# Delta-rule attention with a gated convolution: T's natural layout by identity products on PE, the first group's 16-to-32 step as PE products, and a redrawn order

## The chip, the cores and the metric

The kernel runs on one core of one Trainium2 chip. The metric is device time in microseconds (us) of the whole launch. Shown beside it is the span of the profiled execution, from the first to the last instruction in its trace. PE is the matrix engine (TensorE), DVE the vector engine, ACT the scalar engine, POOL GpSimd, SP the engine that issues the transfers; PEld is PE's weight load.

## The reference

For each of 4 batches and 8 heads a state of 48 x 48 is carried over 768 positions. Each position reads the state with its query, and then corrects the state by a delta rule along its normalised key; the outputs of the heads are put side by side to rows of 384 and go through a gate of a causal convolution of 5 taps, a value product, and an output product.

```python
k_n = k / (norm(k, axis=-1) + 1e-6)
for t in range(S):                                    # S = 768
    y[t]  = q[t] @ state                              # 48 x 48 state per batch and head
    state = state + b[t] * outer(k_n[t], v[t] - k_n[t] @ state)
x = y, heads side by side                             # 4 x 768 x 384
gate = sigmoid(sum over k of conv_w[k] * x[t - 4 + k])
out  = (gate * (x @ w_val)) @ w_out
```

The three weight arrays of the second half arrive as 64-bit floats and are turned to 32 bits on the chip.

## The kernel before

The positions are cut into 12 chunks of 64, and two chunks make a group, so there are 6 groups, numbered 0 to 5. 32 pairs of batch and head are handled at once; in a group there are 32 columns `u`, 16 for each chunk `c` (0 and 1), and each column carries two pairs on the halves of the 128 partitions.

**Preparing a group (`prep`).** `gram` multiplies keys with keys and queries (tile KQ, loaded by SP) on PE, and ACT copies the result to GL. `diag` copies the diagonal 32 x 32 blocks to D1, and a DVE transpose turns them into TLP. `coef` works out the norms and, with the loaded beta (tile BE), the factors CT: its 18th step is the first that reads BE, and everything behind it needs CT. Inside one chunk of 64 the delta rule needs the inverse T of a unit triangular matrix. DVE builds it for blocks of 8 (`row`), merges them to 16 (`mergez8`, `merget8`), and then to 32 (`zmul`, `zred`, `tmul`, `tred`; POOL does a part of the products). All of this has the 128 matrices' entries along the free dimension. `trans_out(0)` then transposes to the layout TTR, and `trans_out(1)` a second time to TNA, the natural (not transposed) layout of T. Last, the step from 32 to 64 is done on PE: `lev1` multiplies GL and TTR into a bank `z`, ACT copies it to ZS (four copies of 32 partitions), `lev2` multiplies TNA and ZS into a bank `t`, and ACT copies it into BD beside two scaled copies of TTR (`bdcopy`).

**Following the state (`chain`).** For each chunk the products `e` (state with keys, KF), `u` (BD with the corrected values VT), `S` (update of the state, kept in the PSUM tiles SPS) and `y` (output) run on PE, with ACT and DVE copying between. `y` goes to XB, a part of it through YS and six small transfers.

**The second half (`moe`).** For each chunk and each of three blocks `m` of 128 features: `conv` does taps 0 and 1 on PE, DVE adds taps 2 to 4 (`tap`), ACT applies the sigmoid, `val` (three products) and `gate` follow, then `out` (two runs of three products), a copy to OS, and the store. POOL copies four positions from one chunk's X to the next (`halo`).

**What sets the order.** All operations are recorded by `plan.add` in a list. They are then issued in the sequence of a table of numbers, `ORDER`; an operation keeps to its place on its engine, since every engine works in order. So a load that stands late in the table stands late in SP's queue. -1 in the table is a `keep_warm`: one product of zeros with zeros into SPS0, which changes no result. The trace shows each 32-bit product as two records, and counts so: 147 keep-warm products are 294 records. The banks of the pool `w` (3 banks: gram, z, t, val, out) and of the pool `c` (3 banks: conv, e, u, y) go round.

The weights of the second half are loaded in seven pieces through two staging slots that lie in other tiles (AQ1, XB1, GTB0), and converted by two ACT, four DVE and two POOL operations each (lines 273 to 290).

## Time and profile before

| | |
|---|---|
| median of 3 runs | 338.1 us (337.85, 338.10, 345.43) |
| profiled execution, own time | 338.18 us |
| its span | 336.5 us |
| busy, share of the span | PE 308.9 us (92%), DVE 261.8 (78%), ACT 193.3 (57%), POOL 124.7 (37%) |
| instructions of the span | 13,878 |
| DMA | 39.47 MB, 117 GB/s in the mean |

The profiled execution's own time is 1.7 us above its span and 0.1 us above the median. A row of the timeline reads: start, duration, engine, line, operation, result <- operands, the shapes, and how many instructions were merged; in square brackets the idle time before it and what ended it. A row of the view by windows reads: the stretch, its length, then for PE, PEld, DVE, ACT and POOL the busy time and the instructions, then the granted PE clock as a share of full speed, the share of the DMA engines' time, and GB/s. A row of the view by groups reads: busy time, mean ns of one instruction, and the idle time before them.

### The profile page before, as it was taken

How to read it: one execution, taken by the hardware profiler on the slowest of the kernel's cores; microseconds unless marked ns; L12 is line 12 of the kernel's file. 1: busy time of each engine (PE TensorE's matmuls, PEld its weight loads, DVE VectorE, ACT ScalarE, POOL GpSimd, SP SyncE). 2: the span in 40 equal slices, each digit the busy share in tenths (PEclk: the TensorE clock that was granted, in tenths of full speed). 3: DMA queues.
4: the chain of work that ended last, by engine and by line, in shares of the span. 5: the costliest groups of instructions: out<-in, count | busy, mean ns of one | idle time of the engine just before them, and what ended most of it. 6: DMA issues, size and time to landing. Idle time of an engine off the chain costs nothing.

```text
span 336.5 us, 13878 instructions
## 1 busy us (share of the span) xinstructions
PE 308.9 (92%) x6050; PEld 251.0 (75%) x6050; DVE 261.8 (78%) x565; ACT 193.3 (57%) x428; POOL 124.7 (37%) x92
## 2 busy tenths in 40 slices
PE   8936999699779979999999999999999999999994
PEld 6835899589757868777787887868776787786872
DVE  5368999999698994999997899896998779511640
ACT  6742402987636865598455897534875633575221
POOL 5441355244980005960057620485200583300000
PEclk9987599755997998999999999999999999999999
DMA  7899805045440573625087664014341742301222
GB/s 213 265 205 262 191 0 158 3 113 170 128 123 1 137 185 113 179 59 159 15 222 209 186 131 150 8 57 131 107 115 37 204 109 79 96 4 27 47 47 47
DMA packets 20283, 39.47 MB, mean 117 GB/s; under 512 B 8112, under 2 KB 11312, under 8 KB 20224
## 3 DMA queue, kind: packets, MB, share of 16 engines
q1 hardware_dynamic: 20224, 38.60, 43.5%
q8 instruction: 47, 0.77, 1.0%
q14 instruction: 12, 0.10, 0.1%
HBM read 32.69 MB, written 4.72 MB: 111 GB/s over the span
## 4 chain that ended last, share of the span: by engine, by line
PE 60%; DVE 14%; ACT 8%; DMA 7%; POOL 4%; issue 3%; SPq 3%; POOLq 0%; ACTq 0%; DVEq 0%
PE out L726 14%; PE val L715 11%; PE conv L700 7%; PE gram L358 4%; PE e L581 4%; PE u L581 3%; PE SPS L769 3%; PE y L649 3%; SPq L221 3%; PE SPS L581 2%; PE y L651 2%; PE z L458 2%; DMA AQ<-in_w_val_dram 2%; PE t L478 2%; DMA X<-YS 2%
## 5 line engine op out<-in xcount | busy, mean ns | idle before, releaser
L705 DVE SCALAR_TENSOR_TENSOR conv<-X,CW,conv 128x256 f32<-128x256 f32 x108 | 49.9, 484 | 14.2 <-PE conv L700 12.1
L715 PE MATMUL val<-X,WV 128*128 128x256 f32 x216 | 52.5, 390 | 0.0
L726 PE MATMUL out<-WO,GT 128*128 128x384 f32 x144 | 50.9, 495 | 0.0
L421 POOL TENSOR_TENSOR PR<-TLP,TT__83 128x768 f32<-128x768 f32 x5 | 10.6, 2118 | 97.0 <-DVE TT__83 L416 97.0
L715 PEld LDWEIGHTS val<-X,WV 128*128 128x128 f32 x216 | 40.3, 192 | 6.9 <-ACT GL L216 0.3
L769 PE MATMUL SPS<-ZW 128*128 128x128 f32 x294 | 43.7, 302 | 0.4 <-ACT US L643 0.4
L769 PEld LDWEIGHTS SPS<-ZW 128*128 128x128 f32 x294 | 39.4, 210 | 5.1 <-issue 3.6
L358 PE MATMUL gram<-KQ 48*64 48x128 f32 x768 | 33.4, 311 | 10.2 <-DMA KQ<-in_kq_dram 8.5
L700 PE MATMUL conv<-X,DW 128*128 128x256 f32 x144 | 37.5, 396 | 2.7 <-POOL X L695 2.3
L726 PEld LDWEIGHTS out<-WO,GT 128*128 128x128 f32 x144 | 26.2, 189 | 15.0 <-DVE GT L719 0.2
L216 ACT ACTIVATE GL<-gram 128x512 f32<-128x512 f32 x48 | 27.1, 596 | 16.7 <-PE gram L358 16.2
L358 PEld LDWEIGHTS gram<-KQ 48*64 48x64 f32 x768 | 26.1, 156 | 13.6 <-issue 9.3
L649 PE MATMUL y<-AQ,US 112*64 112x64 f32 x384 | 31.0, 237 | 4.7 <-issue 4.0
L649 PEld LDWEIGHTS y<-AQ,US 112*64 112x64 f32 x384 | 26.8, 147 | 8.9 <-issue 7.7
L700 PEld LDWEIGHTS conv<-X,DW 128*128 128x128 f32 x144 | 26.5, 194 | 8.4 <-POOL X L695 2.7
L559 POOL TENSOR_SCALAR_AFFINE_SELECT AQ<-GL 64x1024 f32<-64x1024 f32 x24 | 29.2, 1216 | 7.2 <-PE y L649 3.5
L216 ACT ACTIVATE D<-GL 32x512 f32<-32x512 f32 (+1 forms) x36 | 22.6, 628 | 15.8 <-DVE TT__83 L441 15.1
L581 PE MATMUL u<-VT,BD 64*64 64x48 f32 x768 | 30.6, 233 | 0.7 <-DVE VT L633 0.6
L581 PEld LDWEIGHTS u<-VT,BD 64*64 64x64 f32 x768 | 27.7, 148 | 3.8 <-issue 1.1
L651 PE MATMUL y<-AQ,US 128*48 128x64 f32 x384 | 29.1, 233 | 0.0
L633 DVE TENSOR_TENSOR VT<-e,VT 128x384 f32<-128x384 f32 x22 | 12.3, 557 | 20.1 <-PE e L581 14.1
L637 ACT ACTIVATE US<-u 64x384 f32<-64x384 f32 x24 | 11.6, 483 | 27.9 <-PE u L581 27.8
(97 smaller groups left out, 609.7 us busy)
## 6 DMA issues: line engine op xcount, KB each, us to landing
KQ<-in_kq_dram SPq DMA_DIRECT2D x24, 448.0 KB, 5.6
KF<-in_kf_dram SPq DMA_DIRECT2D x11, 448.0 KB, 4.6
KT<-in_kt_dram SPq DMA_DIRECT2D x12, 384.0 KB, 4.2
AQ<-in_qf_dram SPq DMA_DIRECT2D x24, 192.0 KB, 4.5
VT<-in_vt_dram SPq DMA_DIRECT2D x12, 384.0 KB, 4.0
out_dram<-OS SPq DMA_DIRECT2D x48, 96.0 KB, 2.7
AQ<-in_w_val_dram SPq DMA_DIRECT2D x3, 384.0 KB, 6.0
AQ<-in_w_out_dram SPq DMA_DIRECT2D x3, 384.0 KB, 7.6
```

The lines of the kernel that those rows point to most:

```text
L216: A.activation(out=out, in_=in_, func=AF.Copy, **kw)
L358: PE.matmul(bank["g", g, c, 2 * h + s][64 * a:64 * a + 64, 128 * j:128 * (j + 1)], x[:, 0:C], x, start=True, stop=True)
L559: G.affine_select(out=AQ[c][r0:r0 + 64, j], in_=GL[r0:r0 + 64, c * NP:(c + 1) * NP, 64:128], pattern=[[0, NP], [1, C]], compare_op=ALU.is_ ...
L581: return lambda: PE.matmul(*a, stop=True, **k)
L633: V.tensor_tensor(out=v, in0=bank["e", ch, h][:, 0:HB * D].rearrange("p (u x) -> p u x", x=D), in1=v, op=ALU.add)
L649: PE.matmul(p[0:64, C * j:C * j + C], US[ch % 3][0:112, 0, h, D * j:D * j + 64], AQ[c][0:112, 0, pp, :], start=True, stop=True)
L651: PE.matmul(p[64:112, C * j:C * j + C], us[:, 1, h, j, :], AQ[c][:, 1, pp, :], start=True, stop=True)
L700: PE.matmul(p[:, 0:B * C].rearrange("p (b t) -> p b t", t=C), DW[:, m, i, :], x[:, m, :, k:k + C], start=(i == 0), stop=(i == len(PTAPS) - 1))
L705: V.scalar_tensor_tensor(out=p, in0=x[:, m, :, k:k + C], scalar=CW[:, m, k:k + 1], in1=p, op0=ALU.mult, op1=ALU.add)
L715: PE.matmul(p[:, 0:B * C].rearrange("p (b t) -> p b t", t=C), WV[:, k, 128 * m:128 * m + 128], xs[:, k], start=(k == 0), stop=(k == NKT - 1))
L726: PE.matmul(bank["o", ch, i][:, 0:DM], GT[k][:, 2 * i:2 * i + 2, :].rearrange("p b t -> p (b t)"), WO[:, k, :], start=(k == 0), stop=(k == ...
L769: PE.matmul(SPS[0][:, 384:512], ZW, ZW, start=False, stop=True, skip_group_check=True)
```

## The change

T's natural layout is no longer made by DVE's second transpose in groups 1 to 5. PE multiplies blocks of TTR with 32 x 32 pieces of the identity (`lev0`, bank `n`), and ACT copies the bank to TN; there is such a run for each chunk of each group, group 0 too. TN and ZS now hold two halves of 64 partitions, so that one ACT copy of 128 x 256 fills ZS where four of 32 x 256 did, and `lev2` reads and writes on the diagonal places of the array.

In group 0 (`MERGE = (0,)`) DVE stops at blocks of 16. The half-merged T is transposed to TTR and to TNA (so here the second transpose stays), PE multiplies GL with the second half of TTR (`mergew`, 128 products, bank `mw`), DVE turns the bank into WI by a mask and an identity (`mergew_evac`), PE multiplies TNA with WI (`mergeq`, 128 products, bank `mq`), and ACT copies the result into the second half of TTR. The 16-to-32 products of POOL and DVE are gone from this group. POOL builds the two small constants IDH and ML at the start. The other five groups keep DVE's and POOL's 16-to-32 step as it was.

The table `ORDER` is written anew. It holds 86 keep-warm products (147 before). PTAPS stays (0, 1), so that the new branches for no taps on PE are not taken.

```diff
+MERGE = (0,)
 ORDER = [
-    -1, 8, 16, 65, 160, 9, 70, -1, 3, 1, 2, 7, 75, -1, 10, 11, 12, -1, 13, -2, 14, 17, 0, 4, 6, -1, 15, 24, 64, 18,
...
+    -1, 66, 17, 9, 299, 71, 76, 107, 67, 68, 151, 18, 10, 19, 11, 12, 13, 20, 14, 15, 69, 70, 6, 2, 16, 5, 21, 22,
...
+        def mergew(c):
+            if c == 0:
+                bank["mw", g] = wps("mw")
+            for u in range(c * NP, (c + 1) * NP):
+                for r in range(0, 128, 32):
+                    PE.matmul(bank["mw", g][r:r + 32, 16 * u:16 * u + 16], GL[r:r + 32, u, r % 64:r % 64 + 32],
+                              TTR[r:r + 32, u, 16:32], start=True, stop=True, tile_position=(r, r))
+
+        def mergew_evac():
+            V.scalar_tensor_tensor(
+                out=WI, in0=bank["mw", g].rearrange("p (u x) -> p u x", x=16), scalar=ML[:, 0:1],
+                in1=IDH.unsqueeze(1).to_broadcast([128, NU, 16]), op0=ALU.mult, op1=ALU.add)
+
+        def mergeq(c):
+            if c == 0:
+                bank["mq", g] = wps("mq")
+            for u in range(c * NP, (c + 1) * NP):
+                for r in range(0, 128, 32):
+                    PE.matmul(bank["mq", g][r:r + 32, 16 * u:16 * u + 16], TNA[r:r + 32, u, :], WI[r:r + 32, u, :],
+                              start=True, stop=True, tile_position=(r, r))
+
+        def mergeq_evac():
+            copy(A, TTR[:, :, 16:32], bank["mq", g].rearrange("p (u x) -> p u x", x=16))
+
+        def lev0(c):
+            p = bank["n", g, c] = wps("n")
+            for pp in range(NP):
                 u, x = c * NP + pp, 32 * (pp // 2)
                 for r in (0, 64):
-                    to = r + 32 * (pp % 2)
+                    to = 64 * (pp % 2) + r // 2
+                    PE.matmul(p[to:to + 32, x:x + 32], TTR[r:r + 32, u, :], EYE[r:r + 32, r:r + 32],
+                              start=True, stop=True, tile_position=(r, to))
+
+        def nevac(c):
+            copy(A, TN, bank["n", g, c][:, 0:256].rearrange("p (u x) -> p u x", x=32))
...
         def zevac(c):
-            for r in (0, 64):
-                for b in range(2):
-                    copy(A, ZS[r:r + 32, b:NP:2], bank["z", g, c][r + 32 * b:r + 32 * b + 32, 0:256].rearrange("p (u x) -> p u x", x=32))
+            copy(A, ZS, bank["z", g, c][:, 0:256].rearrange("p (u x) -> p u x", x=32))
...
-        def lev2(c, h):
...
+        def lev2(c):
...
                 for r in (0, 64):
-                    to = r + 32 * (pp % 2)
-                    PE.matmul(p[to:to + 32, x:x + 32], TNA[r:r + 32, u, :], ZS[r:r + 32, pp, :],
-                              start=True, stop=True, tile_position=(r, to))
+                    to = 64 * (pp % 2) + r // 2
+                    PE.matmul(p[to:to + 32, 32 * x:32 * x + 32], TN[to:to + 32, x, :], ZS[to:to + 32, x, :],
+                              start=True, stop=True, tile_position=(to, to))
...
+        if g in MERGE:
+            add("DVE", 1.15, trans_out, (0,), r=["TT"], w=["TTR"])
+            add("DVE", 1.15, trans_out, (1,), r=["TT"], w=["TNA"], kind="trans_nat")
...
+            add("ACT", 0.57, mergeq_evac, r=["mq"], w=["TTR"], give="w")
+        else:
...
-        add("DVE", 1.15, trans_out, (1,), r=["TT"], w=["TNA"])
```

Three places of the order. The first is SP's queue at the start. The rows are loads: KQ keys and queries for `gram`, w_val and w_out the weights, BE the beta that `coef` reads in its 18th step. Before, its first rows are these:

```order
L221 DMA AQ_79<-in_conv_w_dram 128x30
L221 DMA AQ_79<-in_w_val_dram 128x768
L221 DMA KQ_67<-in_kq_dram 112x1024
L221 DMA KQ_68<-in_kq_dram 112x1024
L221 DMA BE<-in_beta_dram 128x192
L221 DMA KQ_69<-in_kq_dram 112x1024
L221 DMA AQ_79<-in_w_val_dram 128x768
L221 DMA KQ_67<-in_kq_dram 112x1024
```

And now, from the 13th load to the 23rd (ahead of them stand four KQ, two w_val, the conv weights, two KT, one KF, one VT and one qf):

```order
L224 DMA AQ_79<-in_w_val_dram 128x768
L224 DMA AQ_78<-in_qf_dram 48x1024
L224 DMA KT_71<-in_kt_dram 128x768
L224 DMA KQ_68<-in_kq_dram 112x1024
L224 DMA KQ_67<-in_kq_dram 112x1024
L224 DMA KF_77<-in_kf_dram 112x1024
L224 DMA AQ_79<-in_w_out_dram 128x768
L224 DMA KQ_69<-in_kq_dram 112x1024
L224 DMA KQ_68<-in_kq_dram 112x1024
L224 DMA BE<-in_beta_dram 128x192
L224 DMA KQ_69<-in_kq_dram 112x1024
```

Beta moved from the 5th load to the 22nd, and the third piece of w_val from the 10th to the 13th.

The second place is DVE where group 0's T is finished. Before, the last rows of the 16-to-32 step, the two transposes (TTR, TNA) and group 1's first transpose (TLP) follow each other, with pieces of the weights' conversion (X_99, AQ_79) between:

```order
L441 TENSOR_REDUCE TT__83<-PR 128x16x4
L441 TENSOR_REDUCE TT__83<-D_86 128x16x4
L446 STREAM_TRANSPOSE TTR<-TT__83 128x32x32
L279 SCALAR_TENSOR_TENSOR AQ_79<-AQ_79 128x384
L448 STREAM_TRANSPOSE TNA<-TT__83 128x32x32
L372 STREAM_TRANSPOSE TLP<-D_86 128x32x32
```

Now the rows behind the 8-to-16 step are the transposes. Behind TNA stand ten steps of group 1's `coef` (SS, ROOT and the rows like them) and one row of a weight, and then WI:

```order
L428 TENSOR_REDUCE TT__83<-PR 128x2x8x4
L458 STREAM_TRANSPOSE TTR<-TT__83 128x32x32
L384 STREAM_TRANSPOSE TLP<-D_86 128x32x32
L460 STREAM_TRANSPOSE TNA<-TT__83 128x32x32
L329 TENSOR_SCALAR SS<-TLP 128x32
L331 TENSOR_SCALAR ROOT<-SS 128x32
```

The fourteen rows of the 16-to-32 step that DVE had between `merget8` and TTR are gone, and group 1's transpose stands ahead of TNA.

The third place is ACT between group 0's last copy of T and the first copy of `u` (US_93). Before, from the first bdcopy on:

```order
L467 ACTIVATE BD_91<-TTR,M_119 128x16x32
L216 ACTIVATE BD_91<-t_632 32x8x32 x4
L285 ACTIVATE WO<-AQ_79 128x384
L273 ACTIVATE X_99<-AQ_79 128x384
L467 ACTIVATE BD_91<-TTR,M_116 128x16x32
L216 ACTIVATE GL_80<-gram 128x512
L637 ACTIVATE US_93<-u 64x384
```

Now, from the copy of `mq` to the last of the four copies of `t` that the first `u` needs:

```order
L219 ACTIVATE TTR<-mq 128x32x16
L511 ACTIVATE BD_91<-TTR,M_119 128x16x32
L297 ACTIVATE WO<-AQ_79 128x384 x2
L219 ACTIVATE ZS<-z 128x256
L511 ACTIVATE BD_92<-TTR,M_116 128x16x32
L511 ACTIVATE BD_91<-TTR,M_116 128x16x32
L219 ACTIVATE TN<-n 128x256
L219 ACTIVATE GL_80<-gram 128x512 x2
L219 ACTIVATE DW<-EYE,CW 128x128 x6
L219 ACTIVATE ZS<-z 128x256
L219 ACTIVATE BD_91<-t_937 32x8x32 x4
```

The six copies DW (the taps' weights), which stood among ACT's first ten rows, moved in here, and two copies that the other chunk needs (BD_92, the second ZS) stand ahead of BD_91's.

## The prediction

> **What bounds the kernel now.** I read the page first, then the timeline of each engine over the first 110 us, then the windows, and last the chain of waits for the rest. The page says that PE has work for 92% of the span; its clock row shows tenths of full speed, and is below 8 only in the first 110 us.

> ```profile
> span 336.5 us, 13878 instructions
> ...
> PE 308.9 (92%) x6050; PEld 251.0 (75%) x6050; DVE 261.8 (78%) x565; ACT 193.3 (57%) x428; POOL 124.7 (37%) x92
> ...
> PEclk9987599755997998999999999999999999999999
> ```

> So there are two stages. Up to about 110 us PE waits for the preparation of groups 0 and 1 and is slow; after that it works almost without a gap. The timeline of DVE gives the marks of the first stage: group 0's transpose into TLP, the factors CT (which read beta), the end of the 8-to-16 step (38.79), TTR; then group 1's TLP and TTR.

> ```profile
> 21.49 2.05 DVE L372 STREAM_TRANSPOSE TLP<-D 128x1024 f32<-128x1024 f32 x1 [0.91 <-ACT D L216]
> ...
> 27.91 1.11 DVE L340 SCALAR_TENSOR_TENSOR CT<-BE,QUOT 128x32 f32<-128x32 f32 x1
> 29.05 0.20 DVE L382 COPY TT__83<-CT 128x32 f32<-128x32 f32 x1
> ...
> 38.79 0.96 DVE L421 TENSOR_TENSOR PR<-TLP,TT__83 128x768 f32<-128x768 f32 x1
> ...
> 56.23 2.12 DVE L446 STREAM_TRANSPOSE TTR<-TT__83 128x1024 f32<-128x1024 f32 x1
> ...
> 60.45 1.93 DVE L372 STREAM_TRANSPOSE TLP<-D 128x1024 f32<-128x1024 f32 x1
> ...
> 105.61 2.04 DVE L446 STREAM_TRANSPOSE TTR<-TT__83 128x1024 f32<-128x1024 f32 x1
> ```

> PE's timeline has the answers to them: filling with products of zeros until group 0's TTR is there, the first `z`, the first `u`, and group 1's first `z`.

> ```profile
> 34.12 1.99 PE L358 MATMUL gram<-KQ 48*64 48x128 f32 x32 [3.03 <-DMA KQ<-in_kq_dram]
> ...
> 39.53 18.30 PE L769 MATMUL SPS<-ZW 128*128 128x128 f32 x146
> 58.50 0.74 PE L458 MATMUL z<-TTR,GL 32*32 32x32 f32 x64 [0.67 <-DVE TTR L446]
> ...
> 66.48 1.91 PE L581 MATMUL u<-VT,BD 64*64 64x48 f32 x32
> ...
> 109.95 0.75 PE L458 MATMUL z<-TTR,GL 32*32 32x32 f32 x64
> ```

> **The start: beta.** The 17.4 us between 38.79 and 56.23 (14 rows of the 16-to-32 step, the rest weights) go out of DVE's way. But the order puts beta behind 21 loads. The view by DMA issues gives their sizes, the window from 30 to 40 us a full queue (share 1.02), and ACT's timeline the landing of the second w_out.

> ```profile
> KQ<-in_kq_dram SPq DMA_DIRECT2D x24, 448.0 KB, 5.6
> KF<-in_kf_dram SPq DMA_DIRECT2D x11, 448.0 KB, 4.6
> KT<-in_kt_dram SPq DMA_DIRECT2D x12, 384.0 KB, 4.2
> AQ<-in_qf_dram SPq DMA_DIRECT2D x24, 192.0 KB, 4.5
> VT<-in_vt_dram SPq DMA_DIRECT2D x12, 384.0 KB, 4.0
> ...
> AQ<-in_w_val_dram SPq DMA_DIRECT2D x3, 384.0 KB, 6.0
> ...
> BE<-in_beta_dram SPq DMA_DIRECT2D x1, 96.0 KB, 5.6
> ```

> ```profile
> 30.00:40.00 10.00, 6.97 (x81) 5.93 (x81) 9.30 (x25) 3.06 (x6) 1.17 (x1) 0.65 1.02 238
> ```

> ```profile
> 39.56 0.55 ACT L273 ACTIVATE X<-AQ 128x384 f32<-128x384 f32 x1 [1.86 <-DMA AQ<-in_w_out_dram]
> ```

> Now 8 KQ, 2 KF, 3 KT, 1 VT, 2 qf, 4 pieces of weights and the taps stand ahead of beta: 7,951 KB, with beta 8,047. Before, the KQ that landed at 34.12 was the end of the first 7,151 KB of SP's queue, and the w_out that landed at 39.56 the end of 8,431; that is 235 KB per us, and 8,047 KB fall at 37.9. The early queue is a little fuller now, so I take 37, with 35.5 and 38.5 as ends. DVE wants beta earlier: the third w_val now ends 4,751 KB, between 24 and 25 on the same line; ACT's conversion and `diag` behind it (2.5 us) put TLP at 26.9, and CT 6.4 us later (27.91 - 21.49), at 33.3. So CT waits for beta until 37, which is 9 us later than before.

> The view by groups gives means for what follows.

> ```profile
> L705 DVE SCALAR_TENSOR_TENSOR conv<-X,CW,conv 128x256 f32<-128x256 f32 x108 | 49.9, 484 | 14.2 <-PE conv L700 12.1 <-ACT GT L709 0.7 <-DMA out_dram<-OS 0.3
> ...
> L216 ACT ACTIVATE GL<-gram 128x512 f32<-128x512 f32 x48 | 27.1, 596 | 16.7 <-PE gram L358 16.2
> ...
> L216 ACT ACTIVATE ZS<-z 32x256 f32<-32x256 f32 x48 | 18.0, 375 | 1.9 <-PE z L458 1.0
> L216 ACT ACTIVATE BD<-t 32x256 f32<-32x256 f32 x48 | 17.9, 373 | 3.4 <-PE t L478 2.8
> ...
> L467 ACT ACTIVATE BD<-TTR,M 128x512 f32<-128x512 f32 x24 | 16.9, 720 | 6.4 <-DVE TTR L446 6.2
> ...
> L448 DVE STREAM_TRANSPOSE TNA<-TT__83 128x1024 f32<-128x1024 f32 x6 | 11.9, 1978 | 0.0
> ...
> L285 ACT ACTIVATE WO<-AQ 128x384 f32<-128x384 uint32 x3 | 1.7, 555 | 0.0
> ```

> From there on DVE: CT and a weight row 0.7, then 9.7 for what took from 29.05 to 38.79, three weight rows 1.3: 48.7. TTR 2.1, group 1's TLP 2.1, TNA 2.0, ten steps of `coef` (0.22 each) and a weight row: 57.5. WI is not in the trace; its shape is 128x512 out of PSUM, and the tap's 0.48 for 128x256 bounds it at 0.5 and 1.0; I take 0.8 (nearer to twice the tap): 58.3. `mw` and `mq` are not in the trace either. Each has 256 records, and the nearest row, `z`, needs 0.74 for 64, so 1.4 (moving half as many columns) to 3.0; I take 2.7. `mw` starts when TTR is there (50.8), or when the 100 records of zeros ahead of it are through, 12.5 us at the rate of 39.53's row behind the last gram of about 41.5: 54. It ends at 56.7, hidden under DVE. `mq` ends at 61.0.

> Then ACT's rows in their new order: the copy of `mq` 0.6 (as a gram copy), three bdcopies 2.2, two weights 1.1, ZS, TN and ZS at 0.38 (four times the partitions, the same free size) 1.1, two gram copies 1.2, six DW at no more than a ZS copy's time 2.1, four of `t` 1.5: 9.8, so the first `u` can start near 70.7. It also needs VT, whose scaling now stands on POOL behind a weight that DVE finishes 8 us behind WI; that comes to about the same. From CT to the first `u` it is 33.7 us instead of 38.6, but CT stands 9 us later, and so `u` 4 us later.

> **From the first `u` to group 1.** Two ends race. DVE had 45.2 us from group 1's TLP to its TTR (60.45 to 105.61). That TLP now starts at 50.8; out of the stretch go 11 taps (5.3), 3 gates (1.3) and TNA, in come group 0's TNA and WI (2.8): TTR is done at 92.3. PE had 24.6 us from 66.48 to its first tap product at 91.07, and some of that ran at half clock:

> ```profile
> 91.07 2.87 PE L700 MATMUL conv<-X,DW 128*128 128x256 f32 x12
> ```

> ```profile
> 80.00:82.00 2.00, 2.00 (x44) 1.94 (x44) 1.97 (x3) 1.75 (x5) 0.64 (x1) 0.50 0.30 107
> ```

> The products ahead of group 1's first `n` are the same ones, less a `z` (1.0), and with 16 of `S` (0.9), 4 taps' products (1.9) and 5 of zeros (1.2): 27.6 us, and 70.7 + 27.6 = 98.3. PE is the later, and `n` starts at 98.3; before, `z` stood there at 109.95. [...]

> **From group 1 to the end.** The costs of a run at full clock, and the end, are in the chain of waits:

> ```profile
> 142.56 1.06 PE conv L700 x4
> ...
> 155.55 0.68 PE z L458 x50
> ...
> 159.20 4.07 PE val L715 x18
> ...
> 163.95 4.07 PE out L726 x12
> ...
> 332.17 0.49 ACT OS L216
> ```

> Before, PE took 222.2 us from 109.95 to 332.2. Behind the same point it now has 10 runs of `n` more (as long as `z`: 6.8), and, since it gets there with less done, 8 taps' products (4.2), 9 of `val` (4.1) and 6 of `out` (4.1); it has 19 products of zeros less, 0.2 to 0.4 each (6). That is 13.2 more, 235.4. What it can win are waits. TNA's transpose, 5 times 2.0, leaves DVE, and 9 us of ZS copies leave ACT (48 at 0.375 before, 24 of ZS and TN now), but neither is on PE's way after 110 us: PE's longest loss there is in this window, where y waits 1.9 us and the clock falls.

> ```profile
> 123.00:129.00 6.00, 4.11 (x101) 3.63 (x98) 5.79 (x11) 2.28 (x7) 2.48 (x2) 0.72 0.61 172
> ```

> It loses 6.00 - 4.11 x 0.72 = 3.0 us. With it and some waits of 0.6 us I count 5 us as won (bounds 0 and 8). `lev2` on the diagonal I take at the cost of `t`. So: 98.3 + 235.4 - 5 = 328.7, plus 4.3 from there to the end (336.5 - 332.2), a span of 333.0; with the 1.7 around it 334.7, against 338.18 of this execution and 338.1 in the median. Rounded down for `t`, which may get cheaper: **334 us**. [...]

> **The rivals.**
> First, beta is not late: the queue runs ahead of the line above, or beta passes other loads. For it: its 5.6 us at the start were not more than a KQ's. Against: that is just the time of the 1,391 KB up to its end. CT is then at 33.3, all comes 3.7 us sooner: 330.
> [...]
> Third, no wait is won, and the zeros taken out become idle time: 334 + 5 = 339.
> Fourth, and on the other side: the clock falls in the second stage. 25 products of zeros stood behind group 1's `z` and 6 are left, and `t` has in places a single short run between it and the copies TN and ZS. A fall like that of the last window costs 3.0 us; one for each of the five groups makes 15 us: 349. It decides from the fourth on, at 346. Against: after 130 us several waits of up to 0.7 us left the clock at 9 tenths.

> **How the numbers follow.** Chances: forecast 0.40, first rival 0.15, second 0.20, third 0.13, fourth 0.12. The forecast's own range is 329 to 339 (beta 1.5 either way, `mw`, `mq` and WI 2, won waits 5 to -3). The range, with both quicker rivals together (324) and half of the fourth left out, is 323 to 344. 2% is 6.8 us, about what a measurement of this kernel can tell from no change: faster is below 331.3, slower above 344.9. Faster takes most of the first two rivals and a little of the forecast, 0.37; slower is the fourth, 0.12; the rest 0.51.

> **What would show it.** CT near 37 us with idle time before it that a DMA of beta ends (first step); `mq` ending near 61 and `u` at 71; the clock at 0.5 behind it; group 1's first `n` at 98 with TTR done at 92; the last product near 329. The prediction is wrong if CT stands below 34, if PE's clock is full between 71 and 90, or if PE's idle time after 110 us is more than before.

## The result and the profile after

The changed kernel takes 352.6 us in the median of four runs (349.1 to 357.5); the kernel before took 338.0 on the same chip (336.7 to 345.4). Two of the four runs, the profiled one among them (355.9 us, span 353.9), fell in a slower state of the chip, and all ratios here and below compare fast runs alone. The ratio is 1.035, with a 95% interval of 1.029 to 1.040: the change is slower by 3.5%, about 12 us, where 334 us had been forecast.

The page of the profiled execution, with its clock row, the row for the transfers of instructions, and the engines' shares of the chain that ended last:

```profile
span 353.9 us, 16161 instructions
...
PE 312.7 (88%) x7208; PEld 254.6 (72%) x7208; DVE 240.0 (68%) x547; ACT 182.8 (52%) x405; POOL 120.2 (34%) x106
...
PEclk9557895556986999999899999999999899989999
...
q8 instruction: 56, 0.92, 1.1%
...
PE 80%; DMA 8%; issue 5%; ACT 3%; SPq 2%; DVE 0%; ACTq 0%
```

DVE is busy for 240 us instead of 262 and ACT for 183 instead of 193, so the change unloads what it meant to unload. PE is busy for 4 us more (312.7, was 308.9), and idle for 14 us more. The chain now has 5% "issue", time in which PE waits for nothing that the profile shows.

DVE's marks of the first stage (factors CT, group 0's TTR, group 1's TLP and TTR), in its timeline:

```profile
34.44 0.19 DVE L352 SCALAR_TENSOR_TENSOR CT<-BE,QUOT 128x32 f32<-128x32 f32 x1 [1.70 <-DMA BE<-in_beta_dram]
...
46.01 2.14 DVE L458 STREAM_TRANSPOSE TTR<-TT__83 128x1024 f32<-128x1024 f32 x1
48.05 2.11 DVE L384 STREAM_TRANSPOSE TLP<-D 128x1024 f32<-128x1024 f32 x1
...
93.62 2.09 DVE L458 STREAM_TRANSPOSE TTR<-TT__83 128x1024 f32<-128x1024 f32 x1
```

And PE's answers to them: the last zeros, the new products `mw` and `mq`, the first `z`, the first `u`, group 1's first `n`.

```profile
50.36 1.96 PE L467 MATMUL mw<-TTR,GL 32*32 32x16 f32 x212
54.67 0.83 PE L467 MATMUL mw<-TTR,GL 32*32 32x16 f32 x44 [2.34 <-issue]
55.42 1.65 PE L825 MATMUL SPS<-ZW 128*128 128x128 f32 x6
57.00 2.99 PE L480 MATMUL mq<-WI,TNA 32*32 32x16 f32 x205
61.82 0.93 PE L480 MATMUL mq<-WI,TNA 32*32 32x16 f32 x51 [1.83 <-issue]
63.44 1.08 PE L504 MATMUL z<-TTR,GL 32*32 32x32 f32 x64 [0.69 <-ACT TTR L219]
...
76.50 1.94 PE L632 MATMUL u<-VT,BD 64*64 64x48 f32 x32
...
102.56 0.72 PE L492 MATMUL n<-EYE,TTR 32*32 32x32 f32 x62
```

TTR stands 10.2 us earlier than before (46.0, was 56.2), and still the first `u` is 10.0 us later (76.5, was 66.5). Group 1's first products are 7.4 us earlier (102.6, was 110.0). From there to the end of the last product PE takes 247 us (102.6 to 349.5), where it took 222. In the middle of `mw` and of `mq` PE stands still for about 2 us, with its operands there and no engine to wait for. The view of waits collects such places over the whole span (engine and line, what it waited for, sum, how often, the longest):

```profile
PE u L632 <- issue: 3.0, 2, 2.4
PE SPS L632 <- issue: 2.5, 1, 2.5
PE mw L467 <- issue: 2.3, 1, 2.3
PE t L520 <- issue: 2.2, 3, 1.5
PE n L492 <- issue: 1.9, 1, 1.9
PE mq L480 <- issue: 1.8, 1, 1.8
PE z L504 <- issue: 1.6, 1, 1.6
PE e L632 <- issue: 1.0, 2, 0.8
PE val L768 <- issue: 0.7, 1, 0.7
PE y L700 <- issue: 0.4, 1, 0.4
```

The same view of the kernel before:

```profile
PE y L649 <- issue: 4.0, 3, 1.9
...
PE SPS L581 <- issue: 0.4, 1, 0.4
```

That is 17.4 us against 4.4: 13 us more, about the size of the loss. How much of the loss these waits are is a question for the experiments.

### The profile page after: what moved, and what is told of

It is laid out like the page before. It is cut to its first block, busy times and chain, and to the rows that moved or that the text cites. A ratio compares the mean times of both kernels' runs of the same rounds, so it can differ in the third digit from the quotient of the medians.

```text
span 353.9 us, 16161 instructions
## 1 busy us (share of the span) xinstructions
PE 312.7 (88%) x7208; PEld 254.6 (72%) x7208; DVE 240.0 (68%) x547; ACT 182.8 (52%) x405; POOL 120.2 (34%) x106
## 4 chain that ended last, share of the span: by engine, by line
PE 80%; DMA 8%; issue 5%; ACT 3%; SPq 2%; DVE 0%; ACTq 0%
PE val L768 14%; PE out L779 13%; PE conv L754 10%; PE gram L370 8%; PE SPS L825 6%; PE e L632 6%; PE y L700 4%; PE u L632 4%; PE y L702 3%; PE SPS L632 3%; DMA KQ<-in_kq_dram 3%; PE t L520 3%; PE z L504 2%; PE n L492 2%; DMA AQ<-in_w_val_dram 2%
## 5 line engine op out<-in xcount | busy, mean ns | idle before, releaser
L370 PE MATMUL gram<-KQ 48*64 48x128 f32 x768 | 35.5, 331 | 13.6 <-DMA KQ<-in_kq_dram 9.5
L370 PEld LDWEIGHTS gram<-KQ 48*64 48x64 f32 x768 | 28.4, 167 | 17.6 <-ACT WV L297 6.9
L754 PE MATMUL conv<-X,DW 128*128 128x256 f32 x144 | 38.6, 408 | 2.6 <-DMA X<-YS 2.6
L433 POOL TENSOR_TENSOR D<-TLP,TT__83 128x1024 f32<-128x1024 f32 x5 | 13.1, 2630 | 75.0 <-DVE TT__83 L428 75.0
L779 PEld LDWEIGHTS out<-WO,GT 128*128 128x128 f32 x144 | 27.0, 192 | 15.7 <-issue 0.8
L219 ACT ACTIVATE GL<-gram 128x512 f32<-128x512 f32 x48 | 26.9, 594 | 18.4 <-PE gram L370 18.3
L754 PEld LDWEIGHTS conv<-X,DW 128*128 128x128 f32 x144 | 27.6, 200 | 9.6 <-issue 4.8
L684 DVE TENSOR_TENSOR VT<-e,VT 128x384 f32<-128x384 f32 x22 | 12.2, 555 | 30.7 <-PE u L632 15.8
L700 PE MATMUL y<-AQ,US 112*64 112x64 f32 x384 | 29.2, 231 | 0.5 <-issue 0.4
L700 PEld LDWEIGHTS y<-AQ,US 112*64 112x64 f32 x384 | 25.6, 144 | 5.0 <-issue 3.2
L825 PE MATMUL SPS<-ZW 128*128 128x128 f32 x172 | 28.6, 327 | 0.0
L632 PEld LDWEIGHTS e<-US,KF 48*64 48x64 f32 x704 | 24.7, 140 | 5.3 <-issue 4.6
L632 PE MATMUL e<-US,KF 48*64 48x48 f32 x704 | 27.2, 225 | 1.0 <-issue 1.0
L702 PE MATMUL y<-AQ,US 128*48 128x64 f32 x384 | 27.8, 228 | 0.2 <-DMA AQ<-in_qf_dram 0.2
L825 PEld LDWEIGHTS SPS<-ZW 128*128 128x128 f32 x172 | 25.5, 231 | 2.9 <-issue 2.5
## 6 DMA issues: line engine op xcount, KB each, us to landing
KQ<-in_kq_dram SPq DMA_DIRECT2D x24, 448.0 KB, 5.2
KF<-in_kf_dram SPq DMA_DIRECT2D x11, 448.0 KB, 5.4
KT<-in_kt_dram SPq DMA_DIRECT2D x12, 384.0 KB, 4.5
VT<-in_vt_dram SPq DMA_DIRECT2D x12, 384.0 KB, 4.0
AQ<-in_qf_dram SPq DMA_DIRECT2D x24, 192.0 KB, 3.7
AQ<-in_w_val_dram SPq DMA_DIRECT2D x3, 384.0 KB, 8.4
AQ<-in_w_out_dram SPq DMA_DIRECT2D x3, 384.0 KB, 4.7
```

The costliest lines, as they stand in the source:

```text
L219: A.activation(out=out, in_=in_, func=AF.Copy, **kw)
L370: PE.matmul(bank["g", g, c, 2 * h + s][64 * a:64 * a + 64, 128 * j:128 * (j + 1)], x[:, 0:C], x, start=True, stop=True)
L433: eng.tensor_tensor(out=buf[:, 0:64 * n].rearrange("p (k i j) -> p k i j", k=4, i=16), op=ALU.mult, in0=tl4[:, 1, :, 0, 4 * kb:16].unsquee ...
L632: return lambda: PE.matmul(*a, stop=True, **k)
L700: PE.matmul(p[0:64, C * j:C * j + C], US[ch % 3][0:112, 0, h, D * j:D * j + 64], AQ[c][0:112, 0, pp, :], start=True, stop=True)
L702: PE.matmul(p[64:112, C * j:C * j + C], us[:, 1, h, j, :], AQ[c][:, 1, pp, :], start=True, stop=True)
```

## The theory, and its rival

**Supply theory.** PE's instructions are fetched in pieces. The page counts 56 transfers of instructions with 0.92 MB, 16.4 KB each, and PE has 7,208 products and as many weight loads in the trace: 257 instructions to a piece. Before, it was 47 pieces for 12,100, again 257. The trace has a start time for each piece, and no two of them start less than 3.32 us apart (3.45 in the kernel before). Long products take their time over their instructions: six records of `out` last 2.1 us, so there a piece of 128 records lasts 45 us by estimate, much longer than those 3.3. In a run of 32x32 products a product record and its weight load come every 10.6 ns (0.68 us for the 64 of a `z`, from its start to the next product's), so a piece is used up in 1.35 us, by estimate. The author's estimate was that two or three such runs in a row use up the pieces that are there, and that PE then stands still until the next one comes. The change adds 12 runs of `n` (64 records each), and `mw` and `mq` (256 each), and takes zeros out (2 records each, but 0.22 us long: 131 records fill the 14.6 us from 43.2 to 57.8 in the kernel before).

**Rival.** The waits are chance, or belong to DMA traffic, and the change loses by something else: by beta's place, by the redrawn order, or by the array time of the products added.

## The experiments

Kernels that were run together shared a chip and its runs of the kernel before (the third column).

| kernel | time, us | before, us | ratio | 95% interval |
|---|---|---|---|---|
| changed, once more | 352.3 | 336.9 | 1.047 | 1.035 to 1.059 |
| two units per `n` | 348.7 | 336.9 | 1.038 | 1.029 to 1.047 |
| the same, identity moved twice | 349.4 | 336.9 | 1.038 | 1.030 to 1.046 |
| beta early | 349.9 | 336.9 | 1.042 | 1.032 to 1.051 |
| `n` undone, groups 1 to 5 | 337.2 | 336.7 | 1.006 | 1.001 to 1.011 |
| 16 to 32 undone | 352.3 | 336.7 | 1.044 | 1.026 to 1.061 |
| more zeros ahead of `mq` | 358.3 | 336.7 | 1.072 | 1.054 to 1.090 |
| before, with 10 runs added | 348.6 | 336.7 | 1.043 | 1.035 to 1.052 |
| `n` undone and order mended | 338.4 | 336.9 | 1.006 | 1.001 to 1.011 |
| both undone, redrawn order | 349.4 | 336.9 | 1.041 | 1.030 to 1.051 |
| before, 192 small products | 339.1 | 336.4 | 1.011 | 0.995 to 1.028 |
| before, 384 small products | 353.6 | 336.4 | 1.054 | 1.037 to 1.072 |

### The changed kernel once more

> The changed kernel once more, for a second trace of it. Supply theory (PE's instructions come in pieces of 256, one piece about every 3.5 us at most, and PE stands still where it is through 256 faster than that): the waits of PE that no engine ends fall on the same instructions as in the first trace (inside `mw`, inside `mq`, and at `n`, `z`, `t` or the chain's products behind them), and come to 12 us or more in all. Rival (they are chance, from DMA traffic of that execution): they fall elsewhere, and their sum differs by more than 5 us. Time 349.

Three of the waits in the first trace, and then in the second, by PE's timeline:

```profile
110.02 0.21 PE L492 MATMUL n<-EYE,TTR 32*32 32x32 f32 x1 [1.87 <-issue]
169.14 0.20 PE L632 MATMUL u<-VT,BD 64*64 64x48 f32 x1 [2.39 <-issue]
274.69 0.92 PE L632 MATMUL SPS<-US,KT 64*48 64x48 f32 x32 [2.55 <-issue]
```

```profile
107.01 0.20 PE L492 MATMUL n<-EYE,TTR 32*32 32x32 f32 x1 [2.30 <-issue]
166.23 0.24 PE L632 MATMUL u<-VT,BD 64*64 64x48 f32 x1 [2.67 <-issue]
273.02 0.92 PE L632 MATMUL SPS<-US,KT 64*48 64x48 f32 x32 [1.92 <-issue]
```

All came 1.7 to 3 us earlier in the second execution, and at the same instruction. Counted in the trace's product records, the waits over 0.35 us that "issue" ends stand here:

```
product records ahead of the wait
first trace   604       859  1114  2259  2513  3147  3403  3530  4543  4671              5940  6702
second trace  604  731  859        2259        3147  3403  3530  4543  4671  4925        5940  6702
beta early    604       859        2259  2513  3147  3403  3530  4543  4671        5051  5940  6702
```

Ten of the twelve places of the first trace come back in the second, and eleven with beta early. The differences are close to multiples of 127 (255, 255, 1145 = 9 x 127.2, 254, 634 = 5 x 126.8, 256, 127, ...): 127 products with their weight loads are 254 instructions, one piece by the count of 257 above. The kernel before has its four waits behind 857, 1237, 1869 and 3772 records, 3, 5 and 15 times 127 apart. So the places belong to the program and not to the execution, and the sums by the view of waits are alike: 17.4 us in the first trace, 18.4 in the second, 15.7 with beta early. In `mw` the wait of 2.34 us comes behind 212 records, 1.7 pieces, with long products of zeros ahead of them.

### Two units in one product of `n`, and the same with the identity moved twice

```diff
-            for pp in range(NP):
-                ...
-                    PE.matmul(p[to:to + 32, x:x + 32], TTR[r:r + 32, u, :], EYE[r:r + 32, r:r + 32], ...)
+            for pp in range(0, NP, 2):
+                ...
+                    PE.matmul(p[r:r + 64, x:x + 32], TTR[r:r + 32, u:u + 2, :], EYE[r:r + 32, r:r + 32], ...)
```

In both, `lev1`, `lev2` and the copies of `t` place the halves as the kernel before did, since `n` now lands there. The second kernel writes `p[r:r + 64, x:x + 64]` with the identity broadcast to two copies, and the copy TN reads the first.

> `n` takes two units in one product (64 stationary columns instead of 32): 16 products in each of the 12 runs instead of 32, everything else as in the changed kernel; 192 products and 768 of PE's instructions less, three pieces of 256. Supply theory: each piece less is worth up to 3.5 us where PE waits for pieces; some runs lie where it does not, so 3 to 10 us less, about 343. Rival (the price of `n` is the array's time): 12 runs by half of 0.68 us, 4 us less, about 345. The next kernel tells the two apart.

> As the kernel with two units in one product, but every product of `n` moves the identity twice (64 columns instead of 32, the second copy is not read): as many instructions as that kernel, and the array's time of the changed kernel. Supply theory: as quick as that kernel, within 1.5 us (about 343 to 345). Rival (array time): as the changed kernel, 349.

Both took the same time, 348.7 and 349.4, on ratios of 1.038. That agrees with the supply theory, but it does not tell the theory from its rival, because the two kernels did not differ in what they were to differ in. One run of `n` in the first, and then in the second:

```profile
157.28 1.12 PE L491 MATMUL n<-EYE,TTR 32*64 32x32 f32 x32
157.78 1.15 PE L491 MATMUL n<-EYE,TTR 32*64 32x64 f32 x32
```

From its start to the next product such a run takes 1.05 and 1.08 us wherever the clock is full and no wait lies in it. The changed kernel's runs of 64 records take 0.56 to 1.04. So half as many products with 64 stationary columns cost more of PE's time here, not half of it, and moving 64 columns instead of 32 adds 0.03 us to a run. The gain is 3 us against the changed kernel on that chip (352.3, from two runs), at the low end of 3 to 10, and none against its ratio of 1.035. The waits that "issue" ends did go down, from 17.4 and 18.4 us to 12.9 and 10.5, but the longer runs took some of that back. The pieces now meet at other products, and in the first kernel there are new waits at these (1.5 us at a `y` at 117 us, 2.8 us inside a `z` at 162).

### beta early

> The changed kernel with beta's load moved back to the fifth place of SP's queue. By the profile DVE's CT then stands at 32.7 instead of 34.4 and TTR 1.7 us earlier. Theory: no gain, 349 within 1.5, since PE takes `mw` up only behind its products of zeros, at about 50.4, and TTR was there at 48.2. Rival (beta's place is what the change loses by): all that follows comes 1.7 us or more earlier, 346 to 347.5.

In the profile DVE no longer waits for beta, and TTR's transpose starts at 43.79, 2.2 us earlier than in the changed kernel's first trace. PE does not use it:

```profile
50.13 1.96 PE L467 MATMUL mw<-TTR,GL 32*32 32x16 f32 x212
...
76.19 1.95 PE L632 MATMUL u<-VT,BD 64*64 64x48 f32 x32
```

`mw` and the first `u` stand where they stood (50.4 and 76.5), and 349.9 us is no different from the changed kernel. Beta's place is not what the change loses by, as long as 49 products of zeros stand ahead of `mw`.

### `n` undone for groups 1 to 5

```diff
+NAT = (1, 2, 3, 4, 5)
...
         def trans_out(w):
             if w == 0:
                 V.transpose(out=TTR..., in_=...)
+                if g in NAT:
+                    V.transpose(out=TNA..., in_=tf)
...
         def lev0(c):
+            if g in NAT:
+                return
```

`lev1`, ZS's copies and `lev2` are those of the kernel before in these groups.

> The changed kernel with the identity products `n` undone for groups 1 to 5: there DVE transposes a second time (2.0 us each, 5 more), lev1 and lev2 and the copies ZS are those of the kernel before, no copy TN; group 0 keeps its products. 10 runs of 64 records less: 1,280 of PE's instructions, five pieces of 256. Supply theory: 10 x 0.68 us of runs and most of the 10 us of waits behind group 1's first products go, less what DVE's and ACT's 19 us cost on the way: 12 us less, 337 (334 to 341). Rival (the change loses by its start and by the redrawn order, the identity products cost only their 0.68 us): 349 - 6.8 = 342 or more.

337.2 us, ten runs, 1.006 of the kernel before: nearly the whole loss is gone. It costs DVE five transposes, ACT four copies where two did, and PE gets 10 runs of 64 records less. Against the changed kernel (1.035 in the runs of the result, 1.047 in those of its second trace) that is 10 to 14 us, 1.0 to 1.4 us for each run, where the prediction had 0.68.

### The 16-to-32 step undone

```diff
-MERGE = (0,)
+MERGE = ()
```

In the order, the 17 operations of DVE and POOL stand where group 0's `trans_out(0)` stood, `diag` of group 1 behind them, and 61 more products of zeros where `mw` was.

> The changed kernel with group 0's 16-to-32 step back on DVE and POOL (17 operations, some 17 us, put where the first transpose stood), no `mw` and `mq`; 61 products of zeros more to fill PE until TTR is there, at about 63. Theory: `z` starts at 63 to 64, where it started with the change (mq's copy ended at 63.4), the clock is full there and the first `u` comes at 72 instead of 76.5; DVE is 15 us later with group 1's TTR (about 109 instead of 95.7), which gives that back: 349 to 354 in all. Rival (the step on PE is what gains): `u` at 90 and 360.

352.3 us, a ratio of 1.044, as the changed kernel (1.035 and 1.047), so with the `n` products in place it did not matter where group 0's step is done. In this execution TTR's transpose ended at 57.6 and not at 63 (its first TLP stood at 21.8, where the changed kernel's stood at 24.5: among the kernels in the redrawn order this start differs by up to 4.6 us). `u` came at 74.75 and not at 72, behind a wait of 3.0 us for POOL's VT, which stood in POOL's queue behind a weight. Group 1's TTR was done at 99.4 and not at 109, so the time came out as expected by another way: luck. From TTR's end to `u` the changed kernel takes 28.4 us, this one 17.2: what DVE gains by giving the step to PE, PE takes back.

### More zeros ahead of `mq`

```diff
-..., 313, 314, -3, 130, 131, ...
+..., 313, 314, -12, 130, 131, ...
```

> The changed kernel with 12 products of zeros instead of 3 between `mw` and `mq`. Theory: PE's clock falls at 54 because PE stands still inside `mw` and 32x32 products follow; 9 more full-array products hold it, `mq` starts 1 us later and the stretch from `mq` to the first `u` runs at full clock: `u` at 73 instead of 76.5, 346 in all. Rival (nothing holds it, the stretch is slow for what it is made of): granted clock 0.5 from 56 to 85 as before, `u` at 77.5, 350.

Both were wrong: 358.3 us, 6 us more than the changed kernel's second time (352.3), and `u` at 82.4. The windows show the clock behind it (PE's share is the second column, the granted clock the sixth):

```profile
54.30:61.10 6.80, 5.32 (x65) 5.28 (x66) 5.30 (x23) 0.00 (x0) 0.00 (x0) 0.50 0.01 2
61.10:64.50 3.40, 2.21 (x192) 2.00 (x191) 3.09 (x13) 0.00 (x0) 0.00 (x0) 1.00 0.02 5
64.50:91.80 27.30, 24.27 (x693) 20.93 (x694) 13.43 (x23) 16.02 (x36) 15.58 (x10) 0.50 0.15 43
```

The clock had fallen before the zeros began, so they ran at half speed, 5.0 us for 12. At 61.1, behind them, it was full again. Then `mq` started, stood still for 2.1 us behind record 859, where the pieces meet in the changed kernel too, and the clock was down again for 27 us.

### The kernel before, with ten short runs added

```diff
                     PE.matmul(p[to:to + 32, x:x + 32], GL[r + 32:r + 64, u, 0:32], TTR[r + 32:r + 64, u, :], ...)
+                    if g:
+                        PE.matmul(p[to:to + 32, 256 + x:288 + x], TTR[r + 32:r + 64, u, :],
+                                  EYE[r + 32:r + 64, r + 32:r + 64], ...)
```

> The kernel before with 32 identity products more behind `z`'s own in each of the 10 runs `z` of groups 1 to 5 (into columns of its bank that nobody reads); nothing else is changed, so this adds 1,280 of PE's instructions, five pieces of 256, and 10 x 0.68 us of array time. By array time: 337 + 6.8 = 344. Supply theory: waits of PE that no engine ends appear at these runs, 5 x up to 3.5 us, with falls of the clock behind them: 348 to 355.

348.6 us: 11.9 more than the kernel before, for 6.8 us of array time. A run of 64 records costs 1.19 us in this kernel, measured from the other side and in the old order. Together with the kernel that has `n` undone, which also moves work of DVE and ACT, this shows that such runs cost 1.0 to 1.4 us each, in the old order as in the new.

What the cost is made of bears the supply theory out only in part. The view by windows, from group 1's first `z` or `n` to the end of the last product: the kernel before, this one, the changed kernel, and the one with `n` undone for groups 1 to 5 (PE's busy time is the second column):

```profile
109.95:332.09 222.14, 216.67 (x4629) 170.52 (x4628) 171.68 (x388) 134.61 (x312) 73.50 (x49) 0.99 0.41 107
108.73:343.45 234.72, 225.46 (x5269) 178.63 (x5268) 172.13 (x388) 135.03 (x312) 73.53 (x49) 0.99 0.37 101
102.55:349.51 246.96, 232.75 (x5277) 184.96 (x5276) 174.76 (x399) 129.92 (x298) 76.93 (x53) 0.97 0.37 100
94.08:329.97 235.89, 226.64 (x4637) 179.00 (x4636) 179.48 (x403) 140.13 (x323) 78.55 (x54) 0.97 0.39 107
```

The ten runs added lengthen this stretch by 12.6 us, of which 8.8 are PE's busy time, at the same mean clock, and 3.8 are idle time; the waits that "issue" ends rise by 3.1 (2.3 to 5.4; the longest is 2.0 us, and it stands at a `gram`). The expected waits of up to 3.5 us at five of the runs did not come. Undoing the runs shortens the stretch by 11.1 us: 6.1 of busy time and 5.0 of idle time, in which the waits for instructions fall by 9.4 (12.8 to 3.4) and new waits for ACT take 4 back. Against the changed kernel's second trace it is 13.9 (7.2 busy), and against the one with beta early 7.9 (4.0 busy). So half or more of what a run costs is PE's own time, the rival's array time, and the rest is waiting.

### The order mended, and both parts undone

The first of the two kernels has `n` undone for groups 1 to 5 and the moves that its expectation names. The second has `n` and the 16-to-32 step undone in every group, in the redrawn order.

> An attempt to beat both kernels: the kernel with `n` undone for groups 1 to 5 (337), with group 0's step still on PE, and four moves in the order: beta's load fifth in SP's queue; 33 instead of 49 products of zeros ahead of `mw`, and 1 instead of 3 ahead of `mq`; 10 of them behind `mq`, while ACT copies it, to bring the clock up for the run to the first `u`; the loads of chunk 0's and 1's shifted slices X ahead of three KQ loads of 448 KB; and VT's scaling on POOL ahead of a weight. Theory: `mw` 2 us earlier, the clock up from about 66 instead of 79, one wait for X gone: u at 70, 331 (328 to 335). Rival (the first stage is bound by PE's pieces and the second by PE's work, moves win nothing): 337.

> Both parts of the change undone (16-to-32 step of group 0 on DVE and POOL, second DVE transpose in every group) in the changed kernel's redrawn order, with the moves of X's and VT's loads and scaling, and 97 products of zeros up to `z`: what is left is the order and the layout of where things stand. Theory: 53 fewer long stretches for pieces, the clock full up to `u`, which comes at 70 (VT's scaling no longer waits), DVE late for group 1: 337 to 342. Rival (the redrawn order itself is what loses): 349.

The mended order gave 338.4, no gain over 337.2; its rival was right. Behind `mq` and the zeros that follow it the clock was full from 63.9 to 80.9 in this kernel:

```profile
46.80:63.90 17.10, 10.67 (x355) 9.88 (x355) 15.85 (x53) 2.21 (x4) 3.09 (x3) 0.50 0.05 15
63.90:80.90 17.00, 13.34 (x574) 11.44 (x572) 8.15 (x11) 14.43 (x34) 11.12 (x8) 1.00 0.21 66
```

Even so `u` came at 72.64, 29 us behind `mw` at 43.55. From `mw` to `u` PE reads 1,864 instructions there, 7.3 pieces, and the second window shows what that means at full clock: PE works 13.3 of 17 us. Of the 29 us, 8.2 are waits for instructions, where the changed kernel has 4.7. There it is 1,832 instructions, 7.2 pieces, and the stretch takes 26.1, 26.4, 26.1 and 26.1 us in the changed kernel's two traces, with beta early, and with `n` undone: about 3.65 us a piece, whatever starts earlier. That is no fixed price: here it is 4.0, and with two units in one product of `n` 1,704 instructions take 27.6 us.

With both parts undone the redrawn order takes 349.4, and `u` came at 79.3 and not at 70. That is the number of the rival: in this order the kernel loses 12.5 us without any product of the change. So the order by itself is not harmless; it is drawn for a DVE that has less to do. There DVE is the late one: group 1's second transpose ends at 106.2, and its `z` stands at 106.9. With the step on PE and `n` undone for groups 1 to 5 it stood at 94.1. So in this order the step on PE is worth 12 us when DVE transposes twice, and nothing when it doesn't. Part of that difference is the start (its first TLP stood at 26.4, in the other kernel at 22.7); how the rest divides is not settled.

### The price of a piece by itself

The last two kernels are the kernel before, with small products of zeros in place of 30 of the long ones ahead of group 0's `z`. PE has nothing else to do there, and the products depend on nothing.

```diff
-..., 52, 141, -50, 142, ...
+..., 52, 141, -20, -999, 142, ...
...
+    def tiny():
+        for i in range(96):                      # 48 in the first of the two
+            for r in range(0, 128, 32):
+                PE.matmul(SPS[0][r:r + 32, 384:416], ZW[r:r + 32, 0:32], ZW[r:r + 32, 0:32], start=False,
+                          stop=True, skip_group_check=True, tile_position=(r, r))
```

> The kernel before, with 30 of the 73 products of zeros ahead of group 0's `z` replaced by 192 products of zeros of 32x32 in the four diagonal tiles (the shape of `mw`): three pieces of PE's instructions, at a place where PE has no other work, and where DMA moved 13 GB/s. They start at about 50.3. Array time: 384 records x 10.6 ns = 4.1 us, done at 54.4, before TTR (58.4), `z` as before. Supply theory: the first one or two pieces are there, then PE stands still 2 us or so at every 256 instructions: 7 to 10.5 us, done at 57 to 61.

> The same with 384 such products: three pieces more than with 192. Array time: 4.1 us more, 8.1 us in all, done at 58.4, as long as TTR takes anyway. Supply theory: 3 x 3.5 = 10.5 us more than with 192, so done at 67 to 72, and `z` and all behind it 9 to 13 us late; the waits stand 256 instructions apart, each 2 us or more.

PE's timeline of the kernel with 384:

```profile
48.30 1.60 PE L775 MATMUL SPS<-ZW 32*32 32x32 f32 x166
52.26 1.28 PE L775 MATMUL SPS<-ZW 32*32 32x32 f32 x128 [2.35 <-issue]
58.18 1.93 PE L775 MATMUL SPS<-ZW 32*32 32x32 f32 x128 [4.64 <-issue]
61.91 1.94 PE L775 MATMUL SPS<-ZW 32*32 32x32 f32 x128 [1.80 <-issue]
65.37 1.93 PE L775 MATMUL SPS<-ZW 32*32 32x32 f32 x128 [1.52 <-issue]
68.82 1.35 PE L775 MATMUL SPS<-ZW 32*32 32x32 f32 x85 [1.52 <-issue]
```

128 records are done in 1.28 us at full clock, and the next 128 begin 3.73 us later in the kernel with 192 (53.76 and 57.49). At half clock they are done in 1.93 us, and the next ones begin 3.45 to 3.73 us later (58.18, 61.91, 65.37, 68.82). The expectation has DMA at 13 GB/s here, which is not so for the first part: it moved 108 GB/s from 48.3 to 52.3 and 155 to 58.2, where the one longer step lies (52.26 to 58.18). Behind that it moved 6 GB/s, and the steps are still there, so DMA traffic is not what makes them. The starts of the pieces in the trace have the same step: 55.67, 59.31, 63.06, 66.41, 69.87. The 384 products take 21.6 us where the array needs 8.1 (768 records at 10.6 ns), and the time is 353.6, 17 us more than before. With 192 they take 9.2 us (49.36 to 58.6), end 2.1 us behind TTR (56.5 in that execution), and the time is 339.1, which its interval cannot tell from no change. Three pieces more cost 12.4 us here.

## Why the prediction was wrong

The time lies outside of the range of 323 to 344, and on the other side of the kernel before. Step by step:

**Beta.** Right in its mechanism: CT ended a wait of 1.70 us for beta's DMA. The size was off: 34.4 us and not 37, ahead of the line that was laid through two landings, and ahead of the early end of 35.5. A queue ahead of the line is the first rival's condition, and CT stood nearer to its 33.3 than to 37; what the rival wanted to win by it did not reach `u`.

**DVE up to TTR.** TTR was done at 48.15 and not at 50.8, and that is beta's 2.6 us. The estimate of WI (0.8) measured 0.75.

**`mw`, `mq` and the first `u`.** This step failed, in two places. The 2.7 us were near the time in which `mw`'s products run (1.96 and 0.83), and `mq`'s took 3.9 at half clock; with their waits for instructions the two took 5.1 and 5.8, so `mq` ended at 62.75, not at 61.0, for all that TTR came sooner. And the way from there to `u` was counted as ACT's, 9.8 us. It was PE's own, 13.7 us: `z`, `n`, `gram`, `t` and zeros without a gap worth the name, at half clock. The prediction laid PE's work there at no cost beside ACT. `u` came at 76.5, not at 70.7.

**From `u` to group 1.** 27.6 us were forecast, 26.1 measured, with a wait of 2.6 us for the slices X in it that was not foreseen. DVE's TTR stood at 95.7 (92.3 forecast), and PE was the later, as said. Group 1's `n` thus stood at 102.6, 4.3 us late, all of it from the step before. In the second trace and with beta early the stretch took 21.9 and 22.7 us, without that wait, and `n` stood at 97.9 and 98.9. So there the forecast's 98.3 was met, but by luck: `u` came 5 us late and the stretch was 5 us short.

**From group 1 to the end.** This is the step that turned the sign. Forecast were 235.4 us less 5 won, 230.4; measured 247.0 (249.8 in the second trace, 243.8 with beta early). PE's busy time in it rose by 16.1 us, where 13.2 were forecast, and its idle time by 8.7, from 5.5 to 14.2, where 5 less was forecast; the waits for instructions in it rose by 10.5. The terms for what is moved were not tried apart: the kernel with `n` undone for groups 1 to 5 needs 235.9 there (94.1 to 330.0), where the sum without the 6.8 of `n` gives 228.6, and the 7.3 more stand beside 3.2 us of waits for ACT's copies ZN of `z`, 3.4 us for instructions, and 14 us at half clock (3.4 before). What failed is the price of `n`, "as long as `z`: 6.8". It took the start-to-start time of one run among long products for the whole price of ten runs more. They cost 10 to 14 us by undoing them, and 11.9 by adding them; some 4 to 9 of that is busy time of PE, near the 6.8, and the rest is waiting, which the prediction put at nothing. And "I count 5 us as won" took the wait of 1.9 us at `y` for something that DVE and ACT could relieve; by its place in the count of records (1,869, and 632 since the wait before, 5 x 126.4) it was most likely a wait for a piece of instructions, and of this kind there are 12.8 us in that stretch now, where there were 2.3.

**The rivals.** The fourth had the sign and nearly the number, 349: the clock falls in the second stage. It fell in four windows there, next to the waits for pieces (the last four rows; the first row is the stage before):

```profile
57.00:85.00 28.00, 24.99 (x868) 22.25 (x868) 21.87 (x47) 14.93 (x35) 15.78 (x10) 0.50 0.12 35
108.90:115.80 6.90, 5.78 (x105) 4.82 (x108) 2.56 (x10) 2.67 (x6) 0.00 (x0) 0.51 0.11 17
170.40:173.80 3.40, 3.40 (x65) 3.23 (x64) 2.14 (x7) 2.79 (x6) 0.00 (x0) 0.50 0.37 116
276.20:279.60 3.40, 3.40 (x25) 1.53 (x27) 1.45 (x2) 1.06 (x2) 3.40 (x3) 0.50 0.10 20
310.30:313.70 3.40, 3.40 (x38) 2.37 (x32) 0.34 (x1) 2.22 (x5) 0.00 (x0) 0.50 0.02 5
```

17 us at half clock in that stage cost up to 8.5 us (half of them, an estimate); before there was one such window, 3.4 us. But the rival named the zeros taken out as the cause. Each of the falls comes within 4 us of a long wait for instructions (1.87 us at 108, 2.39 at 167, 2.55 at 272, 1.47 at 308), which makes these the likely cause; the two were not tried apart. A full clock between 71 and 90, which the prediction names as a sign of being wrong, did not come before 85: 0.50 from 57 to 85, by the first row. The 6 us sooner that the 324 in its range and the 0.20 of its second rival count on for a full clock there are shown by no run; with the order mended the clock was full from 63.9 to 80.9, around a `u` at 72.64, and the time was 338.4. The third, no wait won, had the right direction and a third of the size. Of the signs that the prediction named for being wrong, the last came in: PE's idle time after 110 us is 15.8 us, where it was 9.8.

The evidence was in the profile before: a wait of 1.89 us that "issue" ends, at a `y` behind `t`, two products of the chain and a `gram`, with all that `y` reads long there. It was counted among the waits that an unloaded DVE and ACT could win.

## What to carry to other kernels

Where PE runs many small products, count its instructions beside its columns: here every 256 of them (64 products of this kind, 128 records with their weight loads) cost 3.45 to 3.73 us in a stretch that goes on (the kernels with 192 and 384, but for one step of 5.9), so a product of 32 columns has two prices here, 21 ns in front of long products (0.68 us for 32) and 54 to 58 ns behind enough short ones. Replacing one 2 us DVE transpose by two runs of small PE products was a loss here: PE was the bound, and a run cost it 1.0 to 1.4 us. A wait that the profile puts down to "issue" is worth a second look: if it stands at the same instruction in another execution, and multiples of a fixed count apart, the supply of instructions is the likely cause.

No kernel that was run beats the kernel before; with `n` kept to group 0, the change is even with it.
